# A transformer block on one core: seven half-width products in the second down-projection, combined on GpSimd, with LayerNorm in place and transfers spread out

## The chip, the cores and the metric

The kernel runs on one core of one Trainium2 chip. The metric is device microseconds of one execution. The core has TensorE (PE in the profile; PEld is its weight load), VectorE (DVE), ScalarE (ACT), GpSimd (POOL) and SyncE (SP), which issues the transfers. All five run their own instruction streams in order and wait for one another by semaphores.

## The reference

A block with conditioning `c`, an attention over the last 512 cached keys, and a gated feed-forward, on 2048 rows of 512:

```python
mod = (_silu(c) @ w_mod).reshape(c.shape[0], 6, 1, -1)
sa, ca, ga, sb, cb, gb = (mod[:, 0], mod[:, 1], mod[:, 2], mod[:, 3], mod[:, 4], mod[:, 5])
h = _layernorm(x, axis=-1) * (1 + ca) + sa
x = x + ga * _A_ref(h, A_k_cache, A_v_cache, A_wq, A_wo)   # 32 heads of 128, 8 of keys/values, window 512
h = _layernorm(x, axis=-1) * (1 + cb) + sb
x = x + gb * _B_ref(h, B_w_gate, B_w_up, B_w_down)          # (gelu(x @ w_gate) * (x @ w_up)) @ w_down, F = 1792
```

## The kernel before

**Arithmetic.** Every f32 operand is split into a high and a low f16 part, and each product is three matmuls (`mm3`, lines 86 to 88: low x high, high x low, high x high). The query projection and the gate and up projections are made in blocks of 2 x 2 with seven products in place of eight (`PROD`, `COL`, `CHAIN`); the sums of weight blocks are made by GpSimd (`prep_set`), those of activations by `combos`, and partial sums are taken out of the accumulating bank by ACT (`keep`, L785) while the chain goes on. The down-projection is made plainly: `y_tasks` (L840), eight row tiles for each pair of 128 feed-forward columns, each tile two products of 512 columns, then one DVE addition into the f32 tile `acc` (L852).

**Stages.** The 2048 rows go in two halves. Attention runs over 128 units of a head and 512 rows, four steps each, so T = 512 steps `t`: scores, maximum, exponential (`ee`), the two f16 parts (`p`), a DMA transpose into `pt`, and two units later the product with the values (`po`) and the output projection (`py`). Unit 64, at step 256, starts the second half. The order of all engines in this part is written out by hand (`tc.manual_schedule()`), and side work is hung on steps with `at(("w", t), ...)`, `at(("l", t), ...)` for loads, and `sched(...)`, which gives a load its place from the release of the buffers `raw` (five) and `rw` (two).

Into these steps go: the columns of the modulation (`mod_load`, `mod_col`, L131); the LayerNorm of rows of later generations (`ln_tile`, generations 1 to 3, L420), the weight sets for the feed-forward, prepared in the second half and kept in DRAM (`prep_set`, `prep_wd`, `store`, `fetch`), and refetched weights of attention. When a row tile's attention is complete, `attn_final` (L858) stores it as `y1[ti]` and three steps later loads the buffer `acc` with the next. Generation 2, the first half's second LayerNorm, loads `y1` again into a `raw` buffer (`xs`), 32 and more steps after the half, one tile per 13 steps.

**Feed-forward.** After step T come NQ = 28 sets `q` of seven products; set `q = 2n` is the gate and `2n + 1` the up projection of pair `n`. Pairs 0 to 6 are the first pass (first 1024 rows), 7 to 13 the second. `y_next` puts one down-projection tile after products 2, 6, 4 and 3 of each set. Here the order is not written by hand: the compiler's scheduler orders every engine's instructions from the program order and its own estimate of times.

Of the kernel before, what the change touches and what calls it, by code (L numbers as in the profile page):

```python
# [17 lines left out]
P = 128  # L18
# [45 lines left out]
def block_kernel(ctx: ExitStack, tc: tile.TileContext, x, kT, v, wq, wo, wg, wu, wd, cT, wc, wm, out):  # L64
# [25 lines left out]
    acc = {}  # L90

    def load_acc(i, src, eng=nc.sync):
        acc[i] = pool.tile([P, D], F32, tag="acc", name="acc", bufs=2 * QT)
        eng.dma_start(acc[i], src)
# [5 lines left out]
    nc.sync.dma_start(cts, cT)  # L100
    for i in range(QT):
        load_acc(i, rows_of(x, i), nc.scalar if i < 2 else nc.sync)
# [32 lines left out]
    def mod_load(j, dt):  # L135
        t = raw("wmc")
        nc.sync.dma_start(t, wc[j, :, dt, :])
        return lambda: mod_col(j, dt, t, sbc)
# [171 lines left out]
    def store(key, t):  # L310
        KEPT[key] = dram.tile(list(t.shape), F16, name="kept")
        nc.sync.dma_start(KEPT[key], t)

    def fetch(key, t):
        nc.sync.dma_start(t, KEPT[key])
        return t
# [72 lines left out]
    def ln_out(qb, dt):  # L389
# [11 lines left out]
        def affine(act=True):  # L401
# [5 lines left out]
            nc.sync.dma_start(spilled(0, qb)[:, dt, :], st["f"])  # L407
# [12 lines left out]
    def ln_tile(gen, i, src):  # L420
# [4 lines left out]
        def load():  # L425
            st["x"] = raw("xs")
            nc.sync.dma_start(st["x"], src())

        def stat():
            ln_stat(st["x"], st)  # L430
            ln_power(st)

        def norm():
            nc.vector.tensor_scalar(st["x"], st["x"], st["mv"][:, 0:1], st["rs"], op0=ALU.subtract, op1=ALU.mult)
# [6 lines left out]
        def affine(dts):  # L441
            if 0 in dts:
                st["f"] = tmp("hf")
# [5 lines left out]
            if KT - 1 in dts:  # L449
                nc.sync.dma_start(spilled(gen, qb)[:, :, i * P:(i + 1) * P], f.rearrange("p (k q) -> p k q", k=KT))  # L450
# [15 lines left out]
    def combos(gen, p, eng, base=True, d=0, e=0):  # L466
        X = {}

        def load(name):
# [5 lines left out]
            nc.sync.dma_start(X[name], stored(gen, name, p))  # L475
# [54 lines left out]
    def reader(src):  # L530
        st = {}

        def load():
            st["r"] = raw("raw")
            nc.sync.dma_start(st["r"], src)
# [3 lines left out]
    def wo_items(qd, ts_, tp):  # L539
        m = {}  # L540
        for k in range(4):
# [15 lines left out]
            if qd == 0:  # L557
                def load_kept(st=st, sp=sp, src=src):
                    st["r"] = sp["r"] = pool.tile([P, D], F32, tag="wo", name="wor", bufs=8)
                    nc.sync.dma_start(st["r"], src)  # L560
# [121 lines left out]
    def set_load(key, srcs, only=None):  # L682
        for k, src in enumerate(srcs):
            if only in (None, k):
                t = pool.tile([P, 512], F32, tag="rw", name="rw", bufs=NRW)
                nc.sync.dma_start(t, src)
# [87 lines left out]
    def banks(st, tags):  # L774
        def bk(k):
            def get():
                if k not in st:
                    st[k] = bank(*tags[k])
# [79 lines left out]
    def attn_final(ti):  # L858
        y1[ti] = dram.tile([P, D], F32, name=f"y{ti}")
        nc.sync.dma_start(y1[ti], acc[ti])  # L860
        nxt = (ti + 2 * QT) % NT
        at(now[0] + 3, lambda: load_acc(nxt, rows_of(x, nxt) if ti < 2 * QT else y1[nxt]))
# [48 lines left out]
    def early_load(j, dt):  # L911
        nc.sync.dma_start(wct[j][:, dt, :], wc[1, :, dt, :] if j else wm[0, dt])
# [132 lines left out]
    def gate_load(dt):  # L1045
        gps[dt] = raw("wmr")
        nc.sync.dma_start(gps[dt], wm[1, dt])
# [9 lines left out]
    for j, ts_ in ((3, (257, 261, 265, 269)), (4, (259, 263, 267, 271)), (5, (274, 278, 282, 286))):  # L1057
# [5 lines left out]
    at(("w", 272), lambda: mx.update(m=mod_max(3)))  # L1063
    at(274, lambda: mod_scale(3, "mf", 1.0, mx["m"]))
# [24 lines left out]
    plan_gen(2, [T // 2 + 32 + 27 * (i // 2) + 11 * (i % 2) for i in range(8)], 478, 10, lambda i: y1[i])  # L1089
# [11 lines left out]
    for g in range(NG):  # L1101
# [15 lines left out]
        elif half:  # L1117
            for k, pos in ((0, t0 - 18), (3, t0 - 17), (1, t0 - 16), (2, t0 - 15)):
                at(pos, lambda g=g, pr=pr, k=k: set_fetch(g, pr, k))
        if half:  # L1120
            at(t0 - 9, lambda pr=pr: k_fetch(pr))
            if pr % 2 == 0:
                at(t0 + 1, lambda qd=qd: v_fetch(qd))
                for k in range(4):
                    at(t0 + 12 + 2 * k, lambda h=4 * qd + k: wo_fetch(h))
# [19 lines left out]
    B, A, G = {}, {}, {}  # L1145
# [9 lines left out]
    def f_items(q, hold=None):  # L1155
# [27 lines left out]
        def result(key, src):  # L1183
# [3 lines left out]
            else:  # L1187
                g = G.pop((n, key))
                nc.vector.scalar_tensor_tensor(g, g, 0.5 * GU, src, op0=ALU.mult, op1=ALU.mult)
                t = pair("ot", "at", NOT)  # L1190
                nc.scalar.activation(t[:, 0, :], g, AF.Copy)
                nc.vector.tensor_tensor(t[:, 1, :], g, t[:, 0, :], op=ALU.subtract)
                A[n, key] = t
# [29 lines left out]
        tags = {"a": ("s", "fa", 2) if q else ("qa", "fa", 1), "b": ("acc", "fb", NACC), "c": ("acc", "fc", NACC)}  # L1223
        return with_posts(("f", q), 2 + q // (2 * NP), banks(st, tags), after)

# [304 lines left out]
```

## Time and profile before

| | us from the span's start, or as said |
|---|---|
| median of three runs | 1780.09 |
| range of the runs | 1779.77 to 1782.09 |
| profiled execution | 1783.9 |
| its span, first to last instruction | 1782.1 |
| attention, from the first scores to the last transpose issued | 25.7 to 1351.5 |
| down-projection, first to last matmul | 1387.8 to 1777.9 |
| DMA queue of SP, share of the 16 DMA engines' time | 80.0% |

The profile gives for each engine the time in which it executed something. A matmul's recorded duration is its latency, with neighbours overlapping; the distance from one start to the next is its rate. An idle time is put down to what ended it.

### The profile page before, as it was taken

Reading aid. Unit: us, or ns where it says so; the run is one execution under the profiler, and the core shown is the slowest. Engines: PE = TensorE matmul, PEld = TensorE weight load, DVE = VectorE, ACT = ScalarE, POOL = GpSimd, SP = SyncE. Lnnn points to the kernel's source line nnn. Section 1 sums busy time; section 2 is a strip of 40 time slices with the busy share of each in tenths; the row PEclk is TensorE's granted clock in tenths of the full one; section 3 lists DMA queues with packets and bytes.
Section 4 is the critical chain, followed back from the end, with each engine's and each line's share of the span. In section 5 each row is a group of like instructions: output and inputs, shape, how many; then the busy total and the mean of one; then the engine's idle time right before and its main releaser. Section 6 shows DMA issues by size and latency. Waiting matters only on the chain.

```text
span 1782.1 us, 26030 instructions
## 1 busy us (share of the span) xinstructions
PE 1735.6 (97%) x8112; PEld 796.0 (45%) x8114; DVE 1442.5 (81%) x2517; ACT 1211.1 (68%) x2814; POOL 874.2 (49%) x1095
## 2 busy tenths in 40 slices
PE   7899999999999999999999999999999999999999
PEld 5444444444444444444444444444444444444444
DVE  7888888888888888888887888787885758676676
ACT  6877787878878777687877777777773455344342
POOL 4879878776788863236575375464420023000000
PEclk9999999999999999999999999999999999999999
DMA  7999999999999989999999999999985643252321
GB/s 232 197 189 236 204 224 207 222 214 206 218 211 210 211 175 182 228 223 212 217 208 211 237 203 212 212 196 203 187 184 141 215 126 99 73 177 84 86 69 56
DMA packets 663274, 329.71 MB, mean 185 GB/s; under 512 B 553184, under 2 KB 575968, under 8 KB 663136
## 3 DMA queue, kind: packets, MB, share of 16 engines
q1 hardware_dynamic: 662848, 327.53, 80.0%
q8 instruction: 64, 1.05, 0.3%
q14 instruction: 74, 0.61, 0.1%
q10 hardware_dynamic: 288, 0.52, 0.1%
HBM read 133.83 MB, written 59.90 MB: 109 GB/s over the span
## 4 chain that ended last, share of the span: by engine, by line
PE 67%; DVE 14%; ACT 7%; POOL 4%; DMA 4%; issue 4%; SPq 1%; POOLq 0%; ACTq 0%; DVEq 0%
PE py L86 7%; PE py L88 7%; PE py L87 7%; PE ps L86 4%; PE ps L88 4%; PE ps L87 4%; PE po L86 4%; PE po L88 4%; PE po L87 4%; DVE p L901 3%; DVE nm L875 3%; PE fa L86 2%; PE fa L88 2%; PE fa L87 2%; ACT ee L884 2%
## 5 line engine op out<-in xcount | busy, mean ns | idle before, releaser
L884 ACT ACTIVATE ee<-ps,nm 128x512 f32<-128x512 f32 x512 | 350.8, 685 | 244.6 <-DVE nm L875 234.6
L901 DVE SCALAR_TENSOR_TENSOR p<-ee,rr,p 128x512 f16<-128x512 f32 x512 | 464.8, 908 | 0.2
L875 DVE TENSOR_REDUCE nm<-ps 128x1 f32<-128x512 f32 x512 | 348.7, 681 | 67.2 <-PE ps L88 65.8
L896 ACT ACTIVATE p<-ee,rr 128x512 f16<-128x512 f32 x512 | 365.5, 714 | 12.8 <-DMA pt<-p 11.9
L86 PE MATMUL ps<-k,qt 128*128 128x512 f16 x512 | 194.3, 380 | 21.5 <-DVE qt L644 15.2
L86 PE MATMUL po<-pt,v 128*128 128x512 f16 x512 | 194.0, 379 | 2.8 <-DVE p L901 1.3
L86 PE MATMUL py<-wo,ot 128*128 128x512 f16 x512 | 194.1, 379 | 2.1 <-DVE ot L644 2.0
L88 PE MATMUL ps<-k,qt 128*128 128x512 f16 x512 | 194.2, 379 | 0.0
L87 PE MATMUL ps<-k,qt 128*128 128x512 f16 x512 | 194.2, 379 | 0.0
L88 PE MATMUL py<-wo,ot 128*128 128x512 f16 x512 | 194.0, 379 | 0.0
L87 PE MATMUL py<-wo,ot 128*128 128x512 f16 x512 | 194.0, 379 | 0.0
L88 PE MATMUL po<-pt,v 128*128 128x512 f16 x512 | 194.0, 379 | 0.0
L87 PE MATMUL po<-pt,v 128*128 128x512 f16 x512 | 194.0, 379 | 0.0
L892 DVE RECIPROCAL rr<-rr 128x2 f32<-128x2 f32 x256 | 41.5, 162 | 118.0 <-ACT rr L889 116.6
L87 PEld LDWEIGHTS <-w 128*128 128x128 f16 x728 | 71.4, 98 | 91.7 <-issue 7.6
L88 PEld LDWEIGHTS <-w 128*128 128x128 f16 x728 | 71.5, 98 | 86.8 <-issue 1.6
L86 PEld LDWEIGHTS <-w 128*128 128x128 f16 x728 | 71.4, 98 | 86.4 <-issue 1.3
L852 DVE SCALAR_TENSOR_TENSOR acc<-py,dysc,acc 128x512 f32<-128x512 f32 x112 | 81.7, 746 | 34.6 <-PE py L88 32.1
L362 POOL TENSOR_TENSOR rs<-rs,nhalf 128x1 f32<-128x1 f32 x32 | 19.2, 599 | 168.6 <-DVE rs L356 166.0
L884 ACT ACTIVATION_READ_ACCUMULATOR ee<-ps,nm 128x1 f32 x512 | 100.7, 197 | 0.0
L852 DVE SCALAR_TENSOR_TENSOR acc<-py,ysc,acc 128x512 f32<-128x512 f32 x128 | 94.6, 739 | 2.5 <-PE py L88 2.5
L86 PE MATMUL py<-wo,at 128*128 128x512 f16 x224 | 84.9, 379 | 3.0 <-DVE acc L852 1.9
(263 smaller groups left out, 3818.8 us busy)
## 6 DMA issues: line engine op xcount, KB each, us to landing
w<-kept SPq DMA_DIRECT2D x123, 256.0 KB, 3.1
wo<-kept SPq DMA_DIRECT2D x60, 256.0 KB, 3.2
raw<-in_wo SPq DMA_DIRECT2D x56, 256.0 KB, 3.5
kept<-stage SPq DMA_DIRECT2D x56, 256.0 KB, 3.5
kept<-w SPq DMA_DIRECT2D x39, 256.0 KB, 3.3
rw<-in_wq SPq DMA_DIRECT2D x38, 256.0 KB, 3.8
hs<-hf SPq DMA_DIRECT2D x32, 256.0 KB, 2.7
pt<-p SPq DMA_TRANSPOSE x512, 3.6
```

What stands on the lines that cost most here:

```text
L86: nc.tensor.matmul(ps, llo, rhi, start=first, stop=False, skip_group_check=chain)
L87: nc.tensor.matmul(ps, lhi, rlo, start=False, stop=False, skip_group_check=chain)
L88: nc.tensor.matmul(ps, lhi, rhi, start=False, stop=last, skip_group_check=chain)
L362: nc.gpsimd.tensor_tensor(st["rs"], st["rs"], nhalf, op=ALU.pow)
L852: nc.vector.scalar_tensor_tensor(acc[ti], st["p"], by, acc[ti], op0=ALU.mult, op1=ALU.add)
L875: nc.vector.tensor_reduce(nm, E[t]["ps"], axis=AX.X, op=ALU.max, negate=True)
L884: nc.scalar.activation(e, E[t]["ps"], AF.Exp, bias=E[t]["nm"], scale=1.0, accum_out=sm[:, t % 2:t % 2 + 1])
L892: return lambda: nc.vector.reciprocal(r, r)
L896: nc.scalar.activation(p16[:, 0, :], E[t]["e"], AF.Copy, scale=E[t]["r"])
L901: nc.vector.scalar_tensor_tensor(p16[:, 1, :], E[t]["e"], E[t]["r"], p16[:, 0, :], op0=ALU.mult, op1=ALU.subtract)
```

## The change

It consists of these parts.

- For pairs 7 to 12 the down-projection is made by seven products of 256 columns (`y_seven`, `YPROD`) in place of eight of twice that shape for 2 x 2 blocks. `y_sums` makes four sums of gated tiles on GpSimd and splits them, ACT the high and GpSimd the low part. Products marked `keep` are copied by ACT out of the accumulating bank and added to two `acc` tiles by GpSimd; the others are added by DVE, after the next product was issued (`defer`). For pairs after 7, `y_next` runs after every product.
- `wd_combined` makes the combined weights of pairs 0 to 5 during the first pass, with loads and stores issued from GpSimd.
- LayerNorm generation 2 takes the tile in `acc` itself, right after its store, with the normalisation on ACT; the eight loads of `y1` for it go. The modulation's columns 3 and 4 move from steps 257 to 271 to steps 239 to 253.
- Stores may be put off up to six steps, fetches get a window (`within`), and loads an earliest place; `spare` issues one of these at steps that have moved nothing. SP's order is written out by hand in the feed-forward too.
- The chain bank `a` of the feed-forward takes three banks in turn (`chain_tag`) in place of two, and the loads of the second pass's `acc` tiles are put off (`load_later`).

The diff, cut to its core:

```diff
+    def store(key, t, slack=6, eng=None):
         KEPT[key] = dram.tile(list(t.shape), F16, name="kept")
+        if slack and 0 <= now[0] < T - 8:
+            bg.append((now[0] + slack, now[0], len(KEPT), lambda: dma(KEPT[key], t)))
+        else:
+            (eng.dma_start if eng else dma)(KEPT[key], t)
+    def spare(t):
+        bg.sort(key=lambda x: x[:3])
+        while bg and bg[0][0] <= t:
+            bg.pop(0)[3]()
+        while not moved[0]:
+            may = [(x[0], 0, x[3], bg, x) for x in bg if x[1] <= t] + [(q[0][0], 1, q[0][2], q, q[0]) for q in pending.values() if q and q[0][1] <= t]
...
+            if gen == 2:
+                return nc.scalar.activation(st["x"], st["x"], AF.Identity, bias=st["nm"], scale=st["rs"])
...
     def attn_final(ti):
-        at(now[0] + 3, lambda: load_acc(nxt, rows_of(x, nxt) if ti < 2 * QT else y1[nxt]))
+        if ti < 2 * QT:
+            own, steps = ln_tile(2, ti, lambda: acc[ti])
+            own()
+            for d, fn in zip((1, 4, 5, 6, 7, 9, 10), steps):
+                at(("w", now[0] + d), fn)
+            at(now[0] + 9, lambda: load_acc(nxt, rows_of(x, nxt)))
+        else:
+            at(now[0] + 3, lambda: load_acc(nxt, y1[nxt]))
...
-    for j, ts_ in ((3, (257, 261, 265, 269)), (4, (259, 263, 267, 271)), (5, (274, 278, 282, 286))):
+    for j, ts_ in ((3, (239, 243, 247, 251)), (4, (241, 245, 249, 253)), (5, (274, 278, 282, 286))):
...
-            for k, pos in ((0, t0 - 18), (3, t0 - 17), (1, t0 - 16), (2, t0 - 15)):
-                at(pos, lambda g=g, pr=pr, k=k: set_fetch(g, pr, k))
+            for k, hi in ((0, 15), (1, 10), (2, 9), (3, 7)):
+                within(t0 - 18, t0 - hi, lambda g=g, pr=pr, k=k: set_fetch(g, pr, k))
...
+    def y_sums(n):
+        g11, g21, g12, g22 = (R.pop((n, k)) for k in ("11", "21", "12", "22"))
+        nc.gpsimd.tensor_tensor(g22, g12, g22, op=ALU.add)
+        nc.gpsimd.tensor_tensor(g12, g11, g12, op=ALU.subtract)
+        nc.gpsimd.tensor_tensor(g11, g22, g11, op=ALU.subtract)
+        nc.gpsimd.tensor_tensor(g21, g21, g11, op=ALU.subtract)
+        def split(k, src):
...
+            nc.scalar.activation(t[:, 0, :], src, AF.Copy)
+            nc.gpsimd.tensor_tensor(t[:, 1, :], src, t[:, 0, :], op=ALU.subtract)
...
-        tags = {"a": ("s", "fa", 2) if q else ("qa", "fa", 1), "b": ("acc", "fb", NACC), "c": ("acc", "fc", NACC)}
+        tags = {"a": chain_tag, "b": ("acc", "fb", NACC), "c": ("acc", "fc", NACC)}
+    def chain_tag():
+        chains[0] += 1
+        return (("qa", "fa", 1), ("s", "fa", 2), ("s", "fa", 2))[(chains[0] - 1) % 3]
...
+    ctx.enter_context(tc.manual_schedule(engines={mybir.EngineType.SP}))
...
+    YPROD = {1: ("a", "11", 0, 0, "keep", 0, 0), 2: ("b", "21", 1, 0, "add", 0, 0), 5: ("c", "s1", 2, 0, "add", 1, 1),
+             6: ("a", "s2", 3, 1, "keep", 0, 1), 3: ("c", "s4", 1, 1, "add", 0, 1), 7: ("a", "s3", 2, 1, "keep", 1, 1),
+             4: ("a", "22", 3, 0, "add", 1, 0)}
+    def y_seven(n, x):
+        def go(k):
...
+            w, rs = WO["f", n, w], slice(256 * h, 256 * h + 256)
+            for ii in range(2):
+                sl = slice((2 * x + ii) * P, (2 * x + ii + 1) * P)
+                mm3(st[ch][:, 256 * ii:256 * ii + 256], A[n, a][:, 0, sl], A[n, a][:, 1, sl], w[:, 0, rs], w[:, 1, rs], ...)
+        def post(k):
...
+            if what == "keep":
+                src = pool.tile([P, 512], F32, tag="rw", name="yk", bufs=NRW)
+                nc.scalar.activation(src, st[ch], AF.Copy, scale=by)
...
+                if what == "keep":
+                    nc.gpsimd.tensor_tensor(t, t, s_, op=ALU.add)
+                else:
+                    defer.append(lambda t=t, s_=s_: nc.vector.scalar_tensor_tensor(t, s_, by, t, op0=ALU.mult, op1=ALU.add))
+        return [[(lambda k=k: go(k), None), (nop, lambda k=k: post(k))] for k in (1, 2, 5, 6, 3, 7, 4)]
...
+    def wd_combined(n, q):
+        def load(k):
+            st[k] = raw("raw")
+            nc.gpsimd.dma_start(st[k], wd[(2 * n + k) * P:(2 * n + k + 1) * P, :])
...
+    for n in range(NP - 1):
+        wd_combined(n, 2 * n + 3)
...
-            if k in (1, 2, 5, 6):
+            if n > NP or k in (1, 2, 5, 6) or load_later:
                 y_next()
-        if m == 1:
+        if m == 1 and seven(n):
+            f_at(q + 1, 2, lambda n=n: nexty.extend(y_seven(n, 0) + y_seven(n, 1)))
```

More of the change, by code (lines that the diff above doesn't have):

```diff
@@ L1320, in block_kernel @@
         go = pos[0] - ahead
-        go = max(go, released[kind].pop(0) + LDGAP)
+        free = released[kind].pop(0) + LDGAP
         released[kind].append(pos[-1])
-        at(("l", max(min(go, pos[0]), 0)), load)
+        pending[kind].append((max(min(max(go, free), pos[0]), 0), max(free + 3, pos[0] - 9), load))
         for p, fn in zip(pos, steps):
@@ L1416, in block_kernel @@
             run(t)
-            run(("l", t))
+            for q in pending.values():
+                while q and q[0][0] <= t:
+                    q.pop(0)[2]()
             run(("w", t))
+            spare(t)
+            moved[0] = 0
             if t == T + 2:
@@ L1457, in block_kernel @@
+    for n in range(NP - 1):
+        wd_combined(n, 2 * n + 3)
+    for n in range(1, 2 * NP):
+        for k in range(4 if seven(n) else 2):
+            f_at(2 * n + 1, 1 + k if seven(n) else 2 * k, lambda n=n, k=k: WO.update({("f", n, k): fetch(("wd", n % NP, k), get_wo())}))
+    for q in range(3, NQ):
         for k, at_ in ((0, 2), (3, 2), (1, 3), (2, 4)):
```

166 lines of the change are left out of this document (121 added, 45 removed).

## Prediction

> **What bounds the kernel now.** I read the page first (busy shares and the chain that ended last), then the busy time by stage, then the waits of TensorE in the stages where it was not full, then single rows for the price of each operation.
>
> The page: the span, the engines' busy time with instruction counts, and the chain's shares by engine.
>
> ```profile
> span 1782.1 us, 26030 instructions
> PE 1735.6 (97%) x8112; PEld 796.0 (45%) x8114; DVE 1442.5 (81%) x2517; ACT 1211.1 (68%) x2814; POOL 874.2 (49%) x1095
> PE 67%; DVE 14%; ACT 7%; POOL 4%; DMA 4%; issue 4%; SPq 1%; POOLq 0%; ACTq 0%; DVEq 0%
> ```
>
> TensorE is busy 97% of the span and carries 67% of the chain; no other engine comes near on the chain. So the first question is how much TensorE work goes, the second how many of its gaps close or open. By stage (columns: length, then busy us and instructions of PE, weight load, DVE, ACT, POOL; clock, DMA share, GB/s):
>
> ```profile
> core 0: us, PE busy (x) PEld busy (x) DVE busy (x) ACT busy (x) POOL busy (x), PEclk, DMA share, GB/s
> 300.00:500.00 200.00, 199.85 (x947) 91.72 (x945) 173.78 (x320) 162.02 (x411) 152.32 (x202) 1.00 0.98 216
> 640.00:680.00 40.00, 38.99 (x182) 17.48 (x181) 33.81 (x55) 29.34 (x70) 18.45 (x19) 1.00 0.73 142
> 680.00:760.00 80.00, 79.61 (x371) 36.15 (x370) 71.26 (x143) 56.01 (x132) 26.95 (x28) 1.00 1.02 222
> 760.00:1000.00 240.00, 234.41 (x1106) 107.60 (x1105) 202.25 (x365) 186.72 (x462) 133.68 (x177) 1.00 0.97 215
> 1000.00:1300.00 300.00, 296.29 (x1382) 133.63 (x1380) 247.94 (x431) 226.55 (x548) 163.69 (x200) 1.00 0.96 206
> 1340.00:1500.00 160.00, 151.61 (x704) 69.33 (x703) 106.85 (x174) 72.04 (x135) 34.40 (x30) 0.99 0.50 147
> 1500.00:1740.00 240.00, 240.00 (x1114) 108.81 (x1113) 167.19 (x255) 97.46 (x153) 0.00 (x0) 1.00 0.33 98
> 1740.00:1782.00 42.00, 37.82 (x175) 16.67 (x173) 27.83 (x42) 12.11 (x19) 0.00 (x0) 1.00 0.16 57
> ```
>
> From 1500 to 1740, the last of the feed-forward's first pass and most of its second, all is TensorE: 240.00 of 240 us, 1114 matmuls, so 240/1114 = 215.4 ns from one to the next, while POOL does nothing, ACT has 59% free and DVE 30%. In the second pass the change puts its seven products. TensorE lacks 8.4 us at the start of the feed-forward part (1340 to 1500), 5.6 us in 760 to 1000 and 3.7 us in 1000 to 1300. What ended waits there (us in total, times, longest): two rows of TensorE and one of ACT from attention's second half (640 to 1310), then three of TensorE from the feed-forward start:
>
> ```profile
> PE ps L86 <- ACT ee L884: 3.3, 4, 1.6
> PE ps L86 <- ACT p L896: 2.7, 2, 1.8
> ACT p L896 <- DMA pt<-p: 11.3, 14, 1.8
> ...
> PE fa L86 <- ACT fg L785: 2.3, 1, 2.3
> PE py L86 <- DVE acc L852: 1.9, 1, 1.9
> PE fa L86 <- ACT fu L785: 0.8, 1, 0.8
> ```
>
> **Term 1, the seven products (six pairs n = 7 to 12).** Before, a pair costs 84 matmuls for gate and up and 8 x 6 = 48 for the down-projection, 512 columns each. After, the 48 become 2 x 7 x 6 = 84 of 256 columns. The price of one of 256 is not in the trace. The near rows:
>
> ```profile
> L86 PE MATMUL py<-wo,at 128*128 128x512 f16 x224 | 84.9, 379 | 3.0 <-DVE acc L852 1.9 <-DVE at L1192 1.1
> L439 PE MATMUL pln<-ident,xs 128*128 128x128 f32 x96 | 14.5, 273 | 0.3 <-DVE acc L852 0.3
> L88 PEld LDWEIGHTS <-at 128*128 128x128 f16 x224 | 21.9, 98 | 26.4
> 1406.63 0.38 PE L439 MATMUL pln<-ident,xs 128*128 128x128 f32 x2
> ```
>
> 379 ns is a latency; the rate is 215.4. Below, half of that is 107.7 ns. Two f32 transposes back to back span 0.38 us with 273 ns each, so they start 107 ns apart, each with its own weight load: a stream of loads and short passes runs at that rate. Above, if the 98 ns load did not hide at all, 98 + 108 = 206 ns; but it hides wholly beside 512 columns. I take 109 ns, from the transposes, with a little for a fixed part. Then 48 x 0.2154 = 10.34 us becomes 84 x 0.109 = 9.16 us: 1.18 us a pair, **-7.1 us** for six. The pair goes from 28.43 to 27.25 us.
>
> The Trainium skill, "TensorE: Matmul & The Clock Gate", section "Back-to-back issue gap", gives 81 ns per matmul at 128 columns once weight loads are in the stream, against 56 alone, so some 25 ns more; the same sentence gives 131 ns at 512, which this trace's 215.4 ns contradicts. By that rule 84 x 6 x 25 ns = 12.6 us would be added and term 1 would be an estimated 5.5 us loss.
>
> **What must hide behind it.** Prices on the other engines (in the rows with three numbers min/median/max ns, in the others busy us and mean ns):
>
> ```profile
> L478 POOL TENSOR_TENSOR cb<-cb x27: 1262/1271/1781, 103.6 to 1482.6; 128x512 f32<-128x512 f32 x27
> L153 POOL TENSOR_TENSOR w<-rw,w x50: 1152/1160/1721, 52.4 to 741.2; 128x512 f16<-128x512 f32 x50
> L153 POOL TENSOR_TENSOR w<-rw,w 128x512 f16<-128x512 f32 x50 | 66.0, 1320 | 4.2
> L1245 POOL TENSOR_TENSOR rw<-rw x56: 722/728/1280, 784.6 to 1242.1; 128x256 f32<-128x256 f32 x56
> L901 DVE SCALAR_TENSOR_TENSOR p<-ee,rr,p x512: 723/743/1751, 36.6 to 1349.6; 128x512 f16<-128x512 f32 x171
> L1171 DVE SCALAR_TENSOR_TENSOR sq<-sq,fg x42: 678/692/1592, 1355.1 to 1761.6; 128x512 f32<-128x512 f32 x42
> L852 DVE SCALAR_TENSOR_TENSOR acc<-py,dysc,acc 128x512 f32<-128x512 f32 x112 | 81.7, 746 | 34.6 <-PE py L88 32.1 <-DMA x<-kept 1.6
> L785 ACT ACTIVATE fg<-fa 128x512 f32<-128x512 f32 x42 | 24.9, 593 | 51.3 <-PE fa L88 51.3
> L1191 ACT ACTIVATE at<-fg 128x512 f16<-128x512 f32 x56 | 35.1, 627 | 66.1 <-DVE fg L1189 66.0
> ```
>
> POOL gets, per pair, 4 sums (1.271), 4 low parts (1.160) and 12 half-width adds (0.728): 5.1 + 4.6 + 8.7 = 18.4 us of 27.25, from nothing. ACT gets 6 copies of partial sums (0.593) and 3 more high parts (0.627), 5.4 us, on 28.43 x 97.46/240 = 11.5: 17 us. DVE exchanges 8 adds of 0.746 for 16 of half the width (each between 0.373, half, and 0.746; by POOL's 0.728/1.271 about 0.43) and drops one low part: 19.8 - 6.0 + 6.8 - 0.7 = 20 us. None exceeds TensorE, so the cover holds on average. But the rows show two clumps: the same operation is short or, at its maximum, longer by about one operation of the other engine (DVE 723 to 1751, POOL 1152 to 1721). Twelve DVE operations of the pair read two SBUF tiles, 12 x 0.69 = 8.3 us. Were POOL and these wholly exclusive, 18.4 + 8.3 = 26.7 us would still fit in 27.25, by 2%. Attention between 300 and 500 us bears more (DVE 87%, POOL 76%, ACT 81%) and TensorE lost 0.15 us of 200 there. The new wait on TensorE is the accumulating bank that ACT must copy out before the next product enters it; queued behind is all of TensorE. The copy takes 0.593 us, and a product of gate or up (6 x 0.215 = 1.29 us) or of the down-projection (6 x 0.109 = 0.65 us) lies between. The 0.65 alone does not always cover it. But the compiler's scheduler orders TensorE in this part, and moves what is ready into such a place: these are the first and the last of twelve down-projection matmuls in a row, where the code alternates six with six of gate and up.
>
> ```profile
> 1562.50 0.38 PE L86 MATMUL py<-wo,at 128*128 128x512 f16 x1
> 1564.87 0.38 PE L88 MATMUL py<-wo,at 128*128 128x512 f16 x1
> ```
>
> Price 0 to 0.5 us a pair; **+1.0 us** in all, 0 to +3.
>
> The Trainium skill, "SBUF — State Buffer", section "Who interferes with whom", says that a DVE instruction with two SBUF inputs and a GpSimd instruction that reads SBUF exclude each other for the whole instruction. The trace agrees for L901, 723 against 1751 ns; it is the second rival.
>
> **Term 2, weights combined on GpSimd in the first feed-forward pass.** For each of six pairs two loads, two products, four half-width differences, two low parts and three or fewer one-input passes, at most 2 x 1.27 + 4 x 0.73 + 5 x 1.16 = 11.3 us a pair of 28.4, on a POOL that is 34.4 us busy in 1340 to 1500. Its own queue issues 4 DMAs a pair; the trace has none from POOL:
>
> ```profile
> raw<-in_wd SPq DMA_DIRECT2D x14, 256.0 KB, 3.3
> ```
>
> Between nothing and POOL standing still for each landing, 4 x 3.3 = 13 us; both fit. The tiles are wanted six pairs later. The cost can only be indirect: they share five `raw` buffers with the loads of the last LayerNorm generation, and SP's order is now fixed by hand, so a load that waits for a buffer holds the weight sets queued behind it. I count this at nothing inside term 3, up to +4.
>
> **Term 3, start of the feed-forward part.** Of the 8.4 us missing, the chain bank's waits (2.3 + 0.8) meet a third rotating bank, and 1.9 the later `acc` loads. Half of these 5.0 us is about **-2.0**, between -5 and +4 (term 2's queueing).
>
> **Term 4, transfers levelled in attention.** ACT waits 11.3 us in 14 pieces for transposes; of what TensorE loses, 3.3 + 2.7 us hang on ACT. Spreading the fetches and taking eight reloads of `y` out, and the eight LayerNorms out of 760 to 1000, should return some: **-2.5**, between -6 and 0.
>
> **Term 5, LayerNorm in place at the half.** Eight tiles now follow the stores of `y` directly, one per 10 us:
>
> ```profile
> L860 SPq DMA_DIRECT2D y<-acc x8: 529/530/615, 691.4 to 762.8; - x8
> L131 DVE SCALAR_TENSOR_TENSOR wmc<-wmc,sbc x12: 675/681/1156, 687.3 to 761.3; 128x512 f32<-128x512 f32 x12
> L447 ACT ACTIVATE hf<-pln,cols x96: 438/457/488, 245.8 to 1449.8; 128x128 f32<-128x128 f32 x96
> L459 ACT ACTIVATE b<-hf x24: 406/428/439, 251.1 to 1029.2; 128x256 f16<-128x256 f32 x24
> ```
>
> Each brings ACT a normalisation (nearest row 0.627), four affine pieces (0.457) and 1.5 parts (0.428): 3.1 us, 25 us in all, onto 56.0 of 80 us: 81 of 80. And eight of the twelve column products (0.68 and a read-out) move about 18 steps earlier, into 640 to 680, where DVE is 33.8 of 40: +6.1 makes 39.9. Both stretches are just full. I take **+1.5**, between 0 and +6.
>
> **Sum.** -7.1 + 1.0 - 2.0 - 2.5 + 1.5 = -9.1 us. The profiled execution took 1783.9 us (1782.1 and 1.8 around it) and would take 1774.8. It lies 3.8 above the median of the runs, 1780.09, which becomes 1771.0.
>
> **Rivals.** *(a) 256 columns cost more than half.* If a quarter of the 98 ns load stays uncovered, 25 ns a matmul, 84 x 6 x 0.025 = 12.6 us come back: 1783.6, about no change. It decides from 123 ns (10.34/84), where term 1 is nil. For: the 98 ns load is nearly as long as the pass. Against: the transposes at 107 ns. 8%. *(b) POOL and DVE exclude each other until the pair is theirs.* If POOL's operations take their means in attention, as L153 with 1320 ns over a median of 1160, some 15% more (21.2 us), with 8.3 that is 29.5 us against 27.25: 2.2 x 6 = 13.5 us, 1784.5, slower. It decides from 27.25. For: the two clumps. Against: 300 to 500 us, and that means and exclusion count the same wait twice. 10%. *(c) The half switch overfills ACT and DVE*: if only a quarter of ACT's 25 us finds a gap, 18.8 us in place of 1.5, 1788, slower; it decides from 14 us, where the gain is spent and 0.2% more. For: 81 of 80. Against: the work is spread over four steps a tile. 9%. *(d) Only waits change hands*: terms 3 and 4 return nothing, and the copies of partial sums cost 0.7 us a pair: -7.1 + 4.2 + 1.5 = -1.4, 1778.7. 10%.
>
> **How the numbers follow.** The forecast has 63%; its own range, from the terms' bounds taken not all together, is 1764 to 1776. A measurement tells 0.2% (3.6 us) from no change. Faster, below 1776.5: the forecast and a little of (d), 0.65. Same: (a) and most of (d), 0.16. Slower: (b), (c) and the queueing of term 2, 0.19. The range of 1763 to 1784 takes in (a), (d) and the lower edge of (b), and leaves out (c) and the far part of (b).
>
> **What would show it.** PE should have 216 more matmuls (8328); 256-column rows of `py` and of the new chain starting 109 ns apart between products; a second-pass pair of 27.3 us in the busy time by stage with TensorE above 98%. POOL should be near 68% there, with maxima near 1.9 us. Term 3 is right if 1340 to 1500 lacks fewer than 7 us; term 4 if ACT's wait for transposes falls below 6 us; term 5 if TensorE loses no more than 2 us between 640 and 770. It is wrong if the matmuls of 256 columns lie over 123 ns apart, if TensorE waits for ACT's or DVE's part of the down-projection in every pair, or if ACT or DVE shows no gaps at the half while TensorE does.

## Result, and the profile after

The change made the kernel slower: 1799.06 us (median of five runs, 1797.82 to 1800.87) against 1782.09 (1779.77 to 1783.45), ratio 1.0098 with a 95% interval of 1.0086 to 1.0109. The profiled execution took 1799.43 us. The experiments below with a ratio were measured four to twelve times, the others once; the kernel before, measured beside them, lay between 1778.7 and 1788.6 us in all, so a few us between single runs decide little. First the page after: span and engines.

```profile
span 1797.4 us, 26826 instructions
PE 1734.2 (96%) x8328; PEld 818.4 (46%) x8330; DVE 1490.6 (83%) x2551; ACT 1247.0 (69%) x2876; POOL 1080.1 (60%) x1313
```

TensorE has the 8328 matmuls that were expected and is busy as long as before (1734.2 against 1735.6); the span grew by 15.3 us, so it is time in which TensorE stands or runs slowly, not more work. Busy time by stage (columns as in the prediction's table, with a cut at 1540 and one at 1611, where the second pass's six changed pairs run, each from a query of its own; the last line is the kernel before in the stretch that changed most):

```profile
640.00:680.00 40.00, 35.15 (x158) 15.52 (x156) 34.42 (x65) 26.00 (x60) 20.32 (x21) 0.96 0.90 194
680.00:760.00 80.00, 78.57 (x373) 36.39 (x372) 69.36 (x132) 63.73 (x155) 35.55 (x47) 1.00 0.84 179
760.00:1000.00 240.00, 235.88 (x1108) 107.58 (x1107) 203.50 (x354) 187.46 (x456) 123.88 (x164) 1.00 0.97 214
1340.00:1500.00 160.00, 151.16 (x709) 69.53 (x708) 116.36 (x173) 72.00 (x134) 69.43 (x71) 1.00 0.52 163
1500.00:1540.00 40.00, 27.74 (x115) 11.66 (x114) 34.06 (x28) 10.89 (x18) 39.69 (x45) 0.87 0.36 115
1611.00:1797.00 186.00, 176.29 (x1060) 102.76 (x1057) 144.51 (x236) 100.67 (x165) 123.49 (x120) 0.99 0.32 105
...
1500.00:1540.00 40.00, 40.00 (x187) 18.14 (x186) 27.62 (x43) 16.50 (x27) 0.00 (x0) 1.00 0.29 89
```

Two holes stand out. In 1500 to 1540, where TensorE had been busy for all of 240 us, it has 115 matmuls against the 187 before, POOL is full with 39.69 of 40, and the granted clock (the share of TensorE's full clock that the profile records) is 0.87. In 640 to 680 TensorE has 35.15 of 40, at a clock of 0.96. TensorE's waits after, in 1500 to 1600, 640 to 700 and 700 to 800 (us in total, times, longest):

```profile
PE fa L86 <- ACT fg L817: 8.0, 1, 8.0
...
PE ps L86 <- DVE qt L676: 4.8, 1, 4.8
...
PE pln L471 <- ACT acc L465: 5.6, 6, 2.4
```

**The hole at 1525.** The wait is put down to ACT's copy of the chain bank, but that copy takes 0.58 us. It stood in ACT's order behind an activation of `sq`, whose row says what it waited for; VectorE's row gives that producer, and GpSimd's timeline what ran beside it.

```profile
1532.16 0.72 ACT L1240 ACTIVATE sq<-sq,tsc 128x512 f32<-128x512 f32 x1 [7.90 <-DVE sq L1237]
1532.79 0.58 ACT L817 ACTIVATE fg<-fa 128x512 f32<-128x512 f32 x1
...
1525.22 6.91 DVE L1237 SCALAR_TENSOR_TENSOR sq<-sq,fg 128x512 f32<-128x512 f32 x1
...
1523.93 0.59 POOL L320 DMA_DIRECT2D kept<-wdc  x1
1524.53 0.54 POOL L1589 DMA_DIRECT2D raw<-in_wd  x1
1525.08 0.79 POOL L1599 TENSOR_TENSOR raw<-raw 128x256 f32<-128x256 f32 x1
1525.84 1.25 POOL L1596 TENSOR_TENSOR raw<-raw,gs 128x512 f32<-128x512 f32 x1
1527.06 1.14 POOL L157 TENSOR_TENSOR wdc<-raw,wdc 128x512 f16<-128x512 f32 x1
1528.17 0.71 POOL L1599 TENSOR_TENSOR raw<-raw 128x256 f32<-128x256 f32 x1
1528.86 0.61 POOL L156 TENSOR_SCALAR wdc<-raw 128x512 f16<-128x512 f32 x1
1529.45 1.25 POOL L1596 TENSOR_TENSOR raw<-raw,gs 128x512 f32<-128x512 f32 x1
1530.67 0.71 POOL L1599 TENSOR_TENSOR raw<-raw 128x256 f32<-128x256 f32 x1
1531.33 0.59 POOL L320 DMA_DIRECT2D kept<-wdc  x1
```

A VectorE instruction of 0.69 us (median of L1237) lasts 6.91: it outlives seven GpSimd instructions and ends 0.8 us after GpSimd turned to issuing a DMA. None of the six GpSimd instructions that started while it stood there is longer than its own median, so GpSimd never waited for VectorE. TensorE stood from 1525.00 to 1533.42; the granted clock was at half from 1528.5 to 1538.7, and after the stop its matmuls started 427 ns apart for another 5.3 us.

To compare kernels I add up TensorE's lost time: distance between starts of neighbouring matmuls, less 215.4 ns for one of 512 columns and less 109 ns for any other (the few matmuls of one or two columns are charged too much by this, so a sum can come out under 0). Stages are bounded by the score steps of attention and by q, the half pairs of the feed-forward (q = 2n + m; 0 to 13 are the first pass); the expectations below call q 10 and 11 "pairs 10 and 11". Each column is one profiled execution, and the same code differs by some us between two of them (compare steps 240 to 256 after and in wd_in_free_ring).

| lost us | before | after | wd_in_free_ring | moves_by_sp | no_seven | levelled_only | ln_spread_no_seven |
|---|---|---|---|---|---|---|---|
| steps 240 to 256 (columns) | 1.3 | 6.5 | 8.2 | 8.4 | 8.1 | 0.9 | 0.9 |
| steps 256 to 300 (LayerNorm) | 0.7 | 7.2 | 7.7 | 8.2 | 8.2 | 1.1 | 5.2 |
| steps 300 to 400 | 6.5 | -0.5 | -0.5 | -0.5 | -0.5 | 12.2 | 5.2 |
| steps 400 to 511 | 5.4 | 1.0 | 0.1 | 1.7 | 1.0 | 0.8 | 1.7 |
| step 511 to q 10 | 12.2 | 10.9 | 6.3 | 19.1 | 6.6 | 3.7 | 3.5 |
| q 10 to 12 | 0.1 | 15.6 | 2.1 | 0.1 | 0.1 | 0.1 | 0.1 |
| q 16 to the last matmul | 1.0 | 6.0 | 5.9 | 6.3 | 0.4 | 0.4 | 0.4 |
| last matmul to the end (duration) | 3.8 | 5.8 | 6.2 | 5.1 | 3.8 | 3.8 | 4.1 |

### The profile page after: what moved, and what is told of

It is laid out like the page before. It is cut to its first block, busy times and chain, and to the rows that moved or that the text cites. A ratio compares the mean times of both kernels' runs of the same rounds, so it can differ in the third digit from the quotient of the medians.

```text
span 1797.4 us, 26826 instructions
## 1 busy us (share of the span) xinstructions
PE 1734.2 (96%) x8328; PEld 818.4 (46%) x8330; DVE 1490.6 (83%) x2551; ACT 1247.0 (69%) x2876; POOL 1080.1 (60%) x1313
## 4 chain that ended last, share of the span: by engine, by line
PE 65%; DVE 16%; ACT 7%; POOL 5%; issue 4%; DMA 3%; SPq 0%; DVEq 0%; POOLq 0%; ACTq 0%
PE py L86 6%; PE py L87 6%; PE py L88 6%; PE ps L86 5%; PE ps L88 5%; PE ps L87 5%; PE po L86 4%; PE po L88 4%; PE po L87 4%; DVE p L940 3%; DVE nm L914 2%; PE qa L86 2%; PE qa L88 2%; PE qa L87 2%; PE fa L86 2%
## 5 line engine op out<-in xcount | busy, mean ns | idle before, releaser
L884 DVE SCALAR_TENSOR_TENSOR acc<-py,ysc,acc 128x512 f32<-128x512 f32 x128 | 94.6, 739 | 10.9 <-PE py L88 10.9
L233 POOL TENSOR_TENSOR lw<-lw,half__86 128x1 f32<-128x1 f32 x37 | 22.0, 594 | 117.3 <-DVE lw L183 117.2
L86 PEld LDWEIGHTS <-qt 128*128 128x128 f16 x512 | 50.4, 98 | 80.3 <-DVE qt L676 23.8
```

What stands on the lines that cost most here:

```text
L86: nc.tensor.matmul(ps, llo, rhi, start=first, stop=False, skip_group_check=chain)
L233: nc.gpsimd.tensor_tensor(out, out, half_, op=ALU.pow)
L884: nc.vector.scalar_tensor_tensor(acc[ti], st["p"], by, acc[ti], op0=ALU.mult, op1=ALU.add)
```

## Experiments

### What blocks VectorE in the first pass

**wd_in_free_ring**: the combined weights get tiles from a ring (the buffers that one kind of tile takes in turn) that is free there.

```diff
-            st[k] = raw("raw")
+            st[k] = pool.tile([P, 512], F32, tag="rw", name="wdr", bufs=NRW)
```

> The tiles that GpSimd loads and combines in the first feed-forward pass take the two `rw` buffers, free at that time, in place of two of the five `raw` buffers; all else as changed. Theory A (these tiles and the last generation's block differences crowd the five buffers, the work of three pairs piles up and GpSimd then runs without a gap from 1500 to 1540 us, which starves VectorE's instructions with two SBUF inputs, one of them for 6.9 us): the pile dissolves, the 8.2 us stop of TensorE at 1525 us goes, with the half clock behind it 8 to 14 us less in 1500 to 1600. Rival B (the pile is the work of GpSimd itself, whatever buffers it takes): no gap comes back, less than 3 us gained.

1781.24 us, with the kernel before beside it at 1781.14. L1237 and the stretch 1500 to 1540:

```profile
L1237 DVE SCALAR_TENSOR_TENSOR sq<-sq,fg x42: 676/693/1755, 1352.9 to 1754.9; 128x512 f32<-128x512 f32 x42
...
1500.00:1540.00 40.00, 38.47 (x178) 17.01 (x177) 36.41 (x45) 18.02 (x29) 34.10 (x34) 1.00 0.35 115
```

One line is worth 18 us: the longest L1237 falls from 6.91 to 1.76 us, and q 10 to 12 lose 2.1 instead of 15.6. But GpSimd is still 34.10 of 40 us busy there. Counted between its DMA issues, its longest run without a pause in the first pass is longer than any there after (16.6 us, thirteen instructions from 1458.37, against 11.9 us), and no VectorE instruction in it takes over 1.6 us. So a long run of GpSimd arithmetic is not enough to block VectorE; inside this one the two take turns.

**wd_half_the_arithmetic**: the loads, splits and stores stay, the other arithmetic goes.

```diff
-(load(0), load(1)), nop, gate, lambda: scaled(0), lambda: scaled(1), combine,
+(load(0), load(1)), nop, nop, nop, nop, nop,
```

> Leaves out the scaling and the differences of the combined weights (7 of 11 GpSimd operations of a pair in the first pass); loads, the split into two parts and stores stay, as do all orders. Theory A (uninterrupted runs of GpSimd arithmetic starve VectorE): GpSimd has gaps, no VectorE operation over 2 us, TensorE loses under 4 us in 1500 to 1600 in place of 16.5. Rival B (the transfers issued from GpSimd, or SP's fixed order, hold the weights back): the stops stay, over 10 us lost there.

1789.78 us (span 1788.0), 4.7 lost in q 10 to 12, longest VectorE instruction 3.02 us (an L1261; the longest L1237 takes 2.68). Less arithmetic makes the blocked stretches shorter, but does not end them: theory A is right in direction and misses its own signs (no operation over 2 us, under 4 lost).

I then counted in the traces what happens where GpSimd goes without a pause from one two-input instruction to the next while a VectorE instruction with two SBUF inputs stands waiting (tiles of 256 columns or more, VectorE there for at least 0.11 us; in 39 further cases in all traces it had come under 0.08 us before the change, and waited for one instruction more). If GpSimd's run had not begun directly (under 0.1 us) behind a DMA issue of its own, VectorE got in next 820 times of 820 in the thirteen traces other than the next three. If it had, VectorE was passed over 37 times of 44. After, 13 of the 24 issues are followed at once by arithmetic, with the own ring 4. Three runs test this.

**moves_by_sp**: SP issues the 24 moves; the shared ring and the arithmetic stay.

```diff
-            nc.gpsimd.dma_start(st[k], wd[...])
+            dma(st[k], wd[...])
-            store(("wd", n, 2 + k), st["o", k], eng=nc.gpsimd)
+            store(("wd", n, 2 + k), st["o", k])
```

> The 24 moves of the combined weights (12 loads, 12 stores) are issued by SP in place of GpSimd; ring, arithmetic and everything else as in the kernel after. In the traces so far, GpSimd arithmetic that starts within 30 ns of a DMA issue of GpSimd itself kept a VectorE instruction with two SBUF inputs out at 37 of 44 boundaries between two of its instructions; in all other back-to-back runs VectorE got in at 820 of 820. Theory A, GpSimd's own DMA issue directly ahead of its arithmetic does the blocking: no such VectorE instruction takes over 1.9 us, TensorE loses under 4 us in pairs 10 and 11 (15.6 after), and the time falls by 11 to 16 us, to 1783 to 1788, less than the 18 us of the own ring if SP's queue now waits for buffers. Rival B, crowding of independent GpSimd instructions does it whoever issues the moves: instructions of 2.5 us and more stay, pairs 10 and 11 lose over 8 us, time above 1791. Rival C, SP stands still for buffers of the shared ring: TensorE waits for weight tiles from DMA in 1400 to 1560, over 4 us.

1796.34 us, ratio 1.0082 (1.0065 to 1.0099). L1237, then TensorE's waits in 1470 to 1525 and POOL's for the loads in 1340 to 1560:

```profile
L1237 DVE SCALAR_TENSOR_TENSOR sq<-sq,fg x42: 674/693/1729, 1356.9 to 1771.4; 128x512 f32<-128x512 f32 x42
...
PE fa L86 <- ACT u L817: 5.2, 2, 3.2
PE fa L86 <- DMA w<-kept: 2.5, 2, 2.3
...
POOL raw L1596 <- DMA raw<-in_wd: 39.8, 4, 15.2
```

Theory A holds for the mechanism: no two-input VectorE instruction takes over 1.9 us, q 10 to 12 lose 0.1, and B is out. The time is missed by 8 us: step 511 to q 10 lose 19.1 where it was 10.9. Part of that is rival C, though a little under its sign of 4 us: loads in SP's order wait for `raw` buffers, GpSimd stands 39.8 us for its loads, and TensorE waits 3.9 us for weight tiles in 1400 to 1560. More of TensorE's time there, 5.9 us, goes in waits for ACT's copies `u`; what held these is open. The half of attention lost 2.9 more too, but its code is the same: there the half clock lasted 6.83 us in place of 3.41, as it did in wd_in_free_ring.

**loads_by_sp**: only the 12 loads go to SP.

```diff
-            nc.gpsimd.dma_start(st[k], wd[...])
+            dma(st[k], wd[...])
```

> Only the 12 loads are issued by SP, the 12 stores stay with GpSimd. Theory A: the long instructions behind loads (2.83, 2.73, 3.54, 6.91 us after) go; one or two of 2.5 to 3.5 us behind a store may stay; pairs 10 and 11 lose 2 to 7 us, time 1783 to 1790. Rival B (crowding): over 8 us lost there, time above 1791.

1795.94 us; 7.3 lost in q 10 to 12. The time lies 6 us above theory A's, with 3 of these lost at the half, where the code is the same. The blocks behind loads are gone; behind stores two stay, one of 2.13 us and one larger than expected:

```profile
1522.37 4.72 DVE L1261 TENSOR_TENSOR at<-fg,at 128x512 f16<-128x512 f32 x1
```

**break_behind_issue**: a one-column memset written behind each issue.

```diff
+            nc.gpsimd.memset(nhalf, -0.5)
```

> A memset of one column on GpSimd stands directly behind each of its 24 DMA issues (it writes the value that is there already); all else as in the kernel after. Theory A1, it is the instruction right behind the issue that takes the pair of engines' access and the run after it keeps it: with an instruction that reads no SBUF in between, the longest VectorE instruction falls below 1.9 us and pairs 10 and 11 lose under 5 us, time near 1785. A2, the issue sets a state that lasts until GpSimd pauses: the memset changes nothing, the 6.9 us instruction and the 15.6 us stay, time 1797 to 1800.

1802.33 us, and the block is there as after (14.5 lost). It decides nothing between A1 and A2: GpSimd's order is not fixed by hand, and most memsets were moved away (4 of the 24 issues have one next); the issue at 1528.77 is followed at once by arithmetic and then by this:

```profile
1529.46 7.00 DVE L1237 SCALAR_TENSOR_TENSOR sq<-sq,fg 128x512 f32<-128x512 f32 x1
```

With these three traces the count stands at 1047 of 1047 and 48 passed over of 57. In sixteen traces the block never came without GpSimd's own DMA issue directly ahead of its run, and it went where SP issued the moves, so that such an issue brings it about is shown (SP's issuing also changed when GpSimd works, but not that it works without pauses: VectorE stood at 78 such changes there and got in each time). Why it does so, and why VectorE got in 9 times all the same, is open.

### The half

**cols_six_later**: columns 3 and 4 of the modulation six steps later.

```diff
-    ... (3, (239, 243, 247, 251)), (4, (241, 245, 249, 253))
+    ... (3, (245, 249, 253, 257)), (4, (247, 251, 255, 259))
```

> The modulation's columns 3 and 4 stand six steps later than in the changed kernel (245 to 259), all else as changed. Theory A (the 5.0 us stop at 650 us is VectorE waiting for a column's load, which waits for a `raw` buffer that the first generation's block differences still hold until about 649 us): the stop goes, and with it the 3.4 us at half clock behind it, about -6 us in 640 to 680; the rest of attention stays. Rival B (VectorE is simply full there, as the prediction's term 5 said): the stop stays or moves, within 2 us of the changed kernel.

1797.77 us. The 4.8 us stop at 650 is gone (6.5 lost becomes 0.9), so its cause is right. These two rows of the kernel after, of VectorE and of GpSimd, show it: VectorE stood 4.99 us for a column tile, whose load SP could issue only when GpSimd had ended the last use of a `raw` buffer (`cb`); SP waited 0.9 us for that instruction, and GpSimd before it 1.89 us for ACT.

```profile
652.23 0.69 DVE L135 SCALAR_TENSOR_TENSOR wmc<-wmc,sbc 128x512 f32<-128x512 f32 x1 [4.99 <-DMA wmc<-in_wc]
...
648.59 1.16 POOL L367 TENSOR_TENSOR t<-cb,t 128x512 f16<-128x512 f32 x1 [1.89 <-ACT t L363]
```

But steps 256 to 300 now lose 9.8 in place of 7.2, in the waits of `pln` for ACT, and the span is only 1.6 us shorter where 6 were expected.

**turn_two_later**: the later steps of each tile's LayerNorm, and the next load, two steps on.

```diff
-            for d, fn in zip((1, 4, 5, 6, 7, 9, 10), steps):
+            for d, fn in zip((1, 4, 7, 8, 9, 11, 12), steps):
...
-            at(now[0] + 9, lambda: load_acc(nxt, rows_of(x, nxt)))
+            at(now[0] + 11, lambda: load_acc(nxt, rows_of(x, nxt)))
```

> The transposes of the LayerNorm in place, and what follows them, stand two steps later (5 becomes 7), so does the next load; all else as changed. Theory A (TensorE, in order, stands at the transposes because ScalarE's normalisation of one step earlier sits behind that step's exponentials; 6.5 us in seven stops between 717 and 787 us): these stops go, about -6 us. Rival B (ScalarE has too much work in these 80 us, 63.7 us busy): the wait only moves to the scores' exponentials, less than 2 us gained.

1801.37 us. The `pln` waits for ACT vanish and others take their place, most of them for VectorE (TensorE's longest in 680 to 810, then that stretch):

```profile
PE py L86 <- DVE ot L676: 2.1, 1, 2.1
...
680.00:810.00 130.00, 125.48 (x596) 58.43 (x595) 110.68 (x209) 106.75 (x260) 55.13 (x73) 1.00 0.87 188
```

ACT is busy 82%, VectorE 85%. Nothing is gained, as rival B forecast, though at 82% its reason, too much work for ACT, is not shown; what is taken from one place falls due in the next.

### The second pass, and each part alone

**no_seven**: the eight products everywhere, no combined weights.

```diff
-        return NP <= n < 2 * NP - 1
+        return False
-    for n in range(NP - 1):
-        wd_combined(n, 2 * n + 3)
```

> The changed kernel with the plain down-projection in every pair (no seven products, no weights combined on GpSimd); levelled transfers and LayerNorm in place stay. Theory A (the pile of GpSimd work in the first pass costs 16 us and the seven products themselves bring nothing in the second pass, since TensorE's 7 us less are spent on waits and on the end): about 1782 us, within 3 us of the kernel with the combined tiles in their own ring (1781.2), second pass as long as there. Rival B (the seven products gain their 7 us once the pile is gone): about 1788 us.

1778.78 us, ratio 0.9981 (0.9971 to 0.9991). From q 16 to the end it takes 185.3 us, as after (185.9) and before (185.5): seven products gain nothing there, as theory A said. The whole lies 3 us under A's 1782.

**levelled_only**: no_seven, with the old LayerNorm (reload of `y`, old column steps).

```diff
-        if ti < 2 * QT:
+        if False:
...
-    for p in range(2):
-        sched_combos(2, p, 478 + 10 * p)
+    plan_gen(2, [T // 2 + 32 + 27 * (i // 2) + 11 * (i % 2) for i in range(8)], 478, 10, lambda i: y1[i])
```

> As no_seven, and the second LayerNorm of the first half goes back to its reload of `y1`, its steps and the modulation's columns to theirs; only levelling and the third chain bank remain. Theory A (LayerNorm in place costs the half switch 12 us net, and levelling alone closes the gaps of 760 to 1340 us, 11 us): about 1770 us, 10 to 13 us under the kernel before. Rival B (what closed those gaps is that the LayerNorm and its eight loads left them): the gaps return, 1778 us or more.

1780.64 us, ratio 0.9984 (0.9970 to 0.9997). The half is clean (0.9 and 1.1), but steps 300 to 400 lose 12.2. TensorE's waits in 760 to 1000:

```profile
PE ps L86 <- ACT ee L923: 5.7, 2, 3.0
PE ps L86 <- ACT p L935: 3.9, 1, 3.9
```

So those gaps close because the LayerNorms and their loads leave, not by levelling, as rival B said; in steps 400 to 511 levelling may have helped (0.8 against 5.4). LayerNorm in place costs 14 at the half (16.3 with no_seven, 2.0 here) and returns 12.7 behind it, each read from one trace; in the medians it is 1.9 us faster.

**seven_own_ring_old_ln** (seven products with the free ring and the old LayerNorm, restored as in levelled_only) and **seven_till_11** (the same, pairs 7 to 11 alone; only this one has the last two lines):

```diff
+            st[k] = pool.tile([P, 512], F32, tag="rw", name="wdr", bufs=NRW)
...
-        if ti < 2 * QT:
+        if False:
...
-        return NP <= n < 2 * NP - 1
+        return NP <= n < 2 * NP - 2
```

> Seven products with the combined tiles in the free `rw` ring, LayerNorm in place undone, levelling kept. Theory A (second pass neutral): within 2 us of levelled_only, about 1769 us. Rival B (seven products worth 7 us): about 1763 us.

> As seven_own_ring_old_ln, but the last but one pair, 12, is made plainly too, so that no half-width product and no GpSimd addition falls into the tail. Theory A (of what eats the second pass's gain, 2.4 us lie between TensorE's last matmul and the end, where the deferred additions of pair 12 stand in VectorE's queue ahead of the last tiles): 1.2 us of TensorE work come back and about 2.4 go, 1 us faster than seven_own_ring_old_ln. Rival B (the tail is no longer for another reason): 1 us slower.

1784.83 us, ratio 1.0017 (0.9998 to 1.0037), and 1784.09, ratio 1.0020 (1.0001 to 1.0038): no faster than the eight products with the same LayerNorm (1780.64, which the expectation had put at 1769). Leaving pair 12 out brings the end from 5.6 back to 4.0 us, but 17.6 lost in steps 300 to 400, against 12.4 by the same code in the other, hide it; that run decides little.

**half_the_adds**: own ring, every second GpSimd addition to `acc` left out.

```diff
-                    nc.gpsimd.tensor_tensor(t, t, s_, op=ALU.add)
+                    ii or nc.gpsimd.tensor_tensor(t, t, s_, op=ALU.add)
```

> The combined tiles in the free `rw` ring, and every second of the twelve GpSimd additions of a pair left out in the second pass (6 x 0.73 to 0.86 us of some 18 a pair). Theory A (the second pass loses its 7 us because GpSimd, 66% busy and shut out by VectorE in turn, is late with the low parts and holds VectorE): TensorE's lost time from pair 7's end on falls from 5.8 us to under 3, the span to about 1776 us. Rival B (TensorE waits for ScalarE's copies out of its bank): the lost time stays above 5 us, span within 1.5 us of 1779.4.

1779.89 us. From q 16 to the end it takes 182.1 in place of 186.1 us, 3.7 lost in place of 5.9 (under 3 expected) and 1.8 less behind the last matmul: half the additions are worth 4.0 us, more than half of the 7.3 that the second pass with the own ring waits more than before. The total does not show it, because a block came up in the first pass even with the own ring, at another place (GpSimd's issue and the first instruction of its run, then VectorE's):

```profile
1497.52 0.54 POOL L1589 DMA_DIRECT2D wdr<-in_wd  x1
1498.07 1.29 POOL L510 TENSOR_TENSOR cb<-cb 128x512 f32<-128x512 f32 x1
...
1501.05 6.64 DVE L1237 SCALAR_TENSOR_TENSOR sq<-sq,fg 128x512 f32<-128x512 f32 x1
```

It too stands beside a run that began directly behind a DMA issue: the own ring mends the timing, not the cause.

**ln_spread_no_seven** and **ln_spread_seven**: columns six steps later, and each tile's LayerNorm two steps further behind than the one before it; without the seven products, and with them in the own ring.

```diff
-                at(("w", now[0] + d), fn)
-            at(now[0] + 9, lambda: load_acc(nxt, rows_of(x, nxt)))
+                at(("w", now[0] + d + 2 * ti), fn)
+            at(now[0] + 9 + 2 * ti, lambda: load_acc(nxt, rows_of(x, nxt)))
```

> Plain down-projection (as no_seven), LayerNorm in place kept, its steps stretched by two more steps for each further tile (one tile per six steps in place of four), modulation columns 3 and 4 six steps later. Theory A (the half switch stops because ScalarE and VectorE have more work than time in these 80 us; over 120 us it fits): TensorE loses under 5 us between step 240 and step 300 in place of 16, the gaps of 760 to 1340 stay closed: about 1768 us, 0.7% under the kernel before. Rival B (in-order TensorE stands at each transpose, however far apart): 10 us or more still lost there, about 1776 us.

> As ln_spread_no_seven, but with the seven products, their combined tiles in the free `rw` ring. Theory A (seven products neutral or a loss of a little): the same within 3 us, rather slower. Rival B (seven products gain 7 us when nothing else is in the way): 5 us or more faster.

1774.43 us, ratio 0.9954 (0.9940 to 0.9968), and 1777.73, ratio 0.9977 (0.9966 to 0.9987). The first is faster than both kernels, by 0.46% and 24.6 us; the half loses 6.1 (expected under 5), and 5.2 come back in steps 300 to 400. The seven products cost 3.3 us here. By the two traces, whose spans are 5.8 us apart, that lies in the first pass, where their weights are made (10.3 us lost from step 511 to q 12 with them, 3.6 without), and hardly in the second (186.1 us from q 16 to the end, against 185.6).

## Why the prediction was wrong

The forecast was 1771.0 us, and 1799.06 came. The step that failed is **term 2**, "nothing inside term 3, up to +4": it cost 15.5 lost in q 10 to 12, and 18 us in all by the one run of wd_in_free_ring. It counted the moves as time of POOL and found that they fit, which on average they did (POOL is busy 69.43 of 160 us in 1340 to 1500), and looked for an indirect price in SP's order. It did not ask what an issue by GpSimd does to VectorE. Rival (b) had the two engines excluding each other, but in the second pass, as a sum of busy times there; each clump in the trace of before was one operation long, and no trace showed an issue by GpSimd. The Trainium skill, "SBUF — State Buffer", section "Who interferes with whom", says that "Issue order, not op shape, decides who blocks", the loser waiting for one whole instruction; the traces agree in the 1047 cases of turn-taking, and differ behind an issue, where VectorE waited for up to seven.

**Term 1** was right in its own price and mis-sized in what must hide behind it. The 256-column matmuls start 105 to 110 ns apart, as in three that follow one another (start, duration):

```profile
1779.52 0.27 PE L86 MATMUL fa<-wo,at 128*128 128x256 f16 x1
1779.63 0.27 PE L87 MATMUL fa<-wo,at 128*128 128x256 f16 x1
1779.74 0.27 PE L88 MATMUL fa<-wo,at 128*128 128x256 f16 x1
```

So rival (a) is out; the work fell by 6.7 us (7.1 predicted). The 12.6 us more by the rule from the Trainium skill, "TensorE: Matmul & The Clock Gate", section "Back-to-back issue gap", did not come either. But the waits were not +1.0: TensorE lost 5.0 more from q 16 on and the end came 2.0 later, 7.0 together, and the whole is nil. TensorE was busy 94.8% of 1611 to 1797, not 98%. POOL's share there is 66% (68% predicted). Rival (d) came nearest with 4.2 us of waits, but put them on ACT's copies of partial sums. These rows after, of GpSimd's additions and of the sums' low parts, and of TensorE's waits in 1600 to 1797, point at GpSimd:

```profile
L1574 POOL TENSOR_TENSOR acc<-acc,yk 128x256 f32<-128x256 f32 x72 | 60.1, 860 | 44.4 <-ACT yk L1569 44.4
L1207 POOL TENSOR_TENSOR as<-u,as 128x512 f16<-128x512 f32 x12 | 15.7, 1307 | 0.0
...
PE py L86 <- POOL as L1207: 2.6, 3, 1.0
```

An addition takes 860 ns on the mean; its median of 732 is the 728 of the price, and the rest is taking turns with VectorE. TensorE waits for the sums' parts, and half_the_adds shows that the additions in GpSimd's order are the greater part of it.

**Term 3** (-2.0): step 511 to q 10 lost 12.2 before and 10.9 after, so -1.3. Its own test, under 7 us lacking in 1340 to 1500, failed (8.84), since the blocks begin there (2.83 us at 1475.62); with the own ring the same part loses 6.3. **Term 4** (-2.5): -7.0 in steps 300 to 400 and -4.4 in 400 to 511, so -11.4. The sign and the test were right (ACT's wait for transposes is 0.7 us, from 11.3), the size is beyond its bound of -6, and most belongs to the LayerNorms that left, by levelled_only. **Term 5** (+1.5, at most +6) measured +11.7 in steps 240 to 300. It too is outside its bound. Of that 5.2 is the column load waiting for a `raw` buffer, with the half clock behind it, which the prediction did not see. The other 6.5 lie in steps 256 to 300, where TensorE waits for ACT's normalisation (5.6 us of `pln`). The prediction named this place and took a quarter of that. But its sums, 81 of 80 us for ACT and 39.9 of 40 for VectorE, did not come: ACT is busy 63.73 of these 80 us and VectorE 34.42 of those 40, so neither was full, and the LayerNorms reach to 795. That moving their steps moves the waits is shown (turn_two_later), and that spreading them makes these smaller (5.2 in ln_spread_no_seven where cols_six_later has 9.8); what sets their size is open. Rival (c), 1788 by this alone, came nearest in size, 11.7 of its 18.8 us, but not by its reason. Terms 4 and 5 are nearly the same work moved, and cancel: -11.4 + 11.7.

In sum, from lost time and work: 0 for the second pass, -1.3, -11.4, +11.7 and +15.5 make +14.5, and q 12 to 16, not in the table, lost 0.9 more, against 15.3 in the span.

## What to carry to other kernels

Before moving work to an idle engine, ask what each of its instructions, its DMA issues among them, shares with other engines, and whether an engine that feeds the bottleneck then has to wait; a fitting sum of busy times says nothing on it. Before a new load takes a tile from a ring, see who holds those buffers at that time: a full ring made the columns late at the half, and in the first pass it packed the work of several pairs together. A saving on a full TensorE is worth what is left after the engines behind it, so run the saving alone before combining it.

## What the hardware showed

VectorE instructions with two SBUF inputs took turns with GpSimd's two-input instructions in 1047 of 1047 cases, but were passed over in 48 of 57 when GpSimd's run began directly behind a DMA that GpSimd itself issued; the longest stood 7.00 us in place of 0.69. VectorE's instructions with an input in PSUM were never held so (at most 0.81 us in any trace). Issuing such a DMA occupied GpSimd for 0.54 to 0.78 us, with medians of 0.58 for the loads and 0.59 for the stores after. And a stop of TensorE cost more than its length: the granted clock went to half for 3.4 us at the end of the stop at 650 and for 10.2 us from within that at 1525, and 2.8 and 5.3 us of these lay behind the stop, with matmuls 427 ns apart. Between 640 us and the last matmuls the half clock came in stretches of 3.41, 6.83 or 10.24 us in all the traces, and the stop at 650 had 3.41 us of it in some executions and 6.83 in others of the same code.
